# A decode attention kernel: K and V of a head fetched in three pieces instead of four, V's last piece multiplied ahead of the softmax, P transposed behind the next head's first keys

## The chip, the cores and the metric

One core of a Trainium2 chip. The metric is device microseconds of one execution; medians of several executions are given. The profile's **span** is shorter than that: it runs from the program's first instruction to its last.

## The reference

One token passes through attention with a cache of 65,536 keys (32 query heads, 8 key/value heads, 128 wide), then through a small gated feed-forward network.

```python
q = (layernorm(x) @ wq) -> [32 heads, 128]
scores = q . k_cache * 128**-0.5          # 8 x 65536 x 128, bf16
o = softmax(scores) . v_cache             # 8 x 65536 x 128, bf16
h = x + o @ wo
out = h + (sigmoid(layernorm(h) @ w_gate) * (layernorm(h) @ w_up)) @ w_down
```

K and V are 16.8 MB each per head, 268 MB for all eight; with the weights 282.33 MB must be read once.

## The kernel before

K and V travel through a ring of 128 KB a partition, in four slots of 32 KB. A 4 MB block of K is transposed on VectorE in eight chunks of 4 KB a partition (into `ktw`), and TensorE makes scores of it. After a head's four blocks come maxima, exponentials on ScalarE and the transposes of P on VectorE; V's blocks are multiplied in *rounds* of eight matmuls (two chunks each), one head behind. The code below is shortened, with lines joined and parts left out.

```python
order = [("wq", 0)] + [("K", b) for b in range(NR)]           # NR = 4 blocks a head
for b in range(NR, NB):
    order += [("K", b), ("V", b - NR)]
# a load waits until the block that was in its slot is used up:
def freed(ld): return {"wq": "q", "K": f"F{b}", "V": f"PV{b}"}[k]
# ...
if r == NR - 1: softmax(i)                 # TensorE: scores, softmax, then V's block
pv(v)
# ...
P.part = {"dve": ("A4", i)}; transposed(i) # VectorE: P's transposes right after the softmax
```

TensorE's program is a loop whose control its own sequencer runs (544 comparisons with jumps are among that sequencer's records in the trace): registers hold addresses (`p` into P, `v` into the ring), and jumps pick the pieces of code.

```python
label("values", "part")
e.reg_mov(m, NR); e.reg_mov(k, 0); e.reg_mov(v, v_even)
# ... jumps to the section of this part (V0, V1, V2, V3), each with its wait
goto("sums", "values")
pv_regs(e)                                 # 14 addresses from p and v
goto("products", "sums")
section("B")                               # 8 matmuls: one round
e.reg_alu(p, p, 2 * 512, ALU.add)
e.reg_alu(v, v, 2 * 2 * CH, ALU.add)
e.reg_alu(m, m, -1, ALU.add)
e.br_ne(m, 0, on_true="sums", on_false="sums_end")
label("sums_end")
away("br_ne", k, 0, "rest", rest, "products")     # the last round of V's last block, behind its own wait
```

`away(...)` is a comparison with a jump to code that lies elsewhere and comes back. In the last head two more things are done between the blocks of V: the output projection of the first seven heads (a section `L`, 28 matmuls called "rows" here), and a *column step* of four small products that turns its result by 90 degrees.

## Time and profile before

| | kernel before |
|---|---|
| time, median of 3 | 658.43 us (658.34 to 658.81) |
| span of the profiled execution | 657.1 us |
| packets of the data queue (q1) | 10,658 |
| last weights landed | 654.83 us |
| last values done | 644.17 us |

In the groups below, the columns are busy time, mean duration in ns of one, then the idle time ahead of them and what ended it.

```profile
L511 DVE STREAM_TRANSPOSE ktw<-ring 128x1024 f32<-128x1024 f32 x256 | 291.6, 1205 | 128.0 <-DMA ring<-in_A_k_cache_dram 128.0
L431 PE MATMUL PS<-ring,PT_sb 128*32 x1024 | 83.9, 455 | 23.6 <-issue 13.2
```

"issue" is time in which TensorE waited for nothing the profile can name. In views of the profile a q after an engine's name (PEq, PEldq, SPq) marks its sequencer.

### The profile page before, as it was taken

The numbers are of one execution on the slowest core, as the hardware profiler recorded it, in microseconds if no ns is written. First come the engines' busy times: TensorE is split into PE (matmuls) and PEld (weight loads), VectorE is DVE, ScalarE is ACT, GpSimd is POOL, SyncE is SP. The second block draws the span as 40 slices with busy tenths as digits, with TensorE's granted clock in tenths as the row PEclk, the third lists the DMA queues.
The fourth block names the chain that finished last, engine by engine and source line by source line (L and its number), as shares of the span: only waits on it lengthen the run. The fifth ranks groups of instructions, "written<-read, shape, count | busy, mean of one in ns | idle before, by whom it ended". The sixth has DMA issues, their size and how long they took to land. (4 is left out here: it accounts for less than half of the span.)

```text
span 657.1 us, 6111 instructions
## 1 busy us (share of the span) xinstructions
PE 420.5 (64%) x2315; PEld 74.1 (11%) x1547; DVE 349.7 (53%) x439; ACT 42.9 (7%) x114; POOL 3.6 (1%) x17
## 2 busy tenths in 40 slices
PE   0688488548666585576765575764866668556746
PEld 0200011011000010010100110101100001001322
DVE  2399775547537665347555374465743575542202
ACT  1100200020000200020000200002000100002001
POOL 1000000000000000000000000000000000000000
PEclk9989689677888697776966769765888869677676
DMA  9999999999999999999999999999999999999998
GB/s 383 447 433 429 439 423 431 431 447 415 447 415 447 437 425 447 415 447 419 443 441 421 447 415 447 423 439 443 419 447 415 447 427 435 445 417 427 435 430 352
DMA packets 10802, 282.34 MB, mean 430 GB/s; under 512 B 1329, under 2 KB 1330, under 8 KB 1842
## 3 DMA queue, kind: packets, MB, share of 16 engines
q1 hardware_dynamic: 10658, 282.33, 99.7%
q10 hardware_dynamic: 144, 0.00, 0.0%
HBM read 282.33 MB, written 0.00 MB: 430 GB/s over the span
## 5 line engine op out<-in xcount | busy, mean ns | idle before, releaser
L431 PE MATMUL PS<-ktw 128*128 128x512 bf16 x1024 | 299.9, 442 | 157.4 <-DVE ktw L511 153.6
L511 DVE STREAM_TRANSPOSE ktw<-ring 128x1024 f32<-128x1024 f32 x256 | 291.6, 1205 | 128.0 <-DMA ring<-in_A_k_cache_dram 128.0
L431 PE MATMUL PS<-ring,PT_sb 128*32 x1024 | 83.9, 455 | 23.6 <-issue 13.2
L431 PEld LDWEIGHTS PS<-ktw 128*128 x256 | 27.1, 106 | 408.2 <-issue 256.8
L565 DVE STREAM_TRANSPOSE PT_sb<-P_sb 128x512 bf16<-128x512 bf16 x32 | 20.2, 684 | 54.0 <-PE PS L602 52.3
L551 ACT ACTIVATE negmax<-PS 128x1 f32<-128x1 f32 x8 | 1.4, 171 | 520.6 <-PE PS L549 520.6
L431 PEld LDWEIGHTS PS<-ring,PT_sb 128*32 x1024 | 25.8, 116 | 79.8 <-issue 74.6
L516 DVE TENSOR_REDUCE M_sb<-PS 128x1 f32<-128x512 f32 x32 | 19.9, 684 | 25.5 <-PE PS L431 25.5
L555 ACT ACTIVATE P_sb<-PS,negmax 128x512 bf16<-128x512 f32 x32 | 21.6, 686 | 0.3
L572 DVE TENSOR_REDUCE lsum<-PS 128x1 f32<-128x4 f32 x8 | 1.3, 163 | 31.2 <-PE PS L570 31.2
L542 PE MATMUL PS<-identf,gm 128*1 128x128 f32 x16 | 3.4, 301 | 16.9 <-DVE gm L540 16.9
L616 DVE TENSOR_TENSOR Lw<-O,blk_of 128x896 bf16<-128x896 bf16 (+1 forms) x2 | 1.4, 683 | 20.6 <-ACT O L606 20.6
L402 PE MATMUL PS<-st,onesf 128*128 128x2 f32 x4 | 1.2, 362 | 16.1 <-DVE st L401 16.1
L431 PE MATMUL PS<-ring,xz 128*8 x32 | 9.2, 459 | 2.3 <-issue 2.3
L599 ACT ACTIVATE po_sb<-PS,rl 128x512 bf16<-128x512 f32 x8 | 5.5, 687 | 53.2 <-PE PS L431 53.2
L431 PE MATMUL PS<-ktw,O 128*1 x26 | 7.6, 464 | 0.0
L549 PE MATMUL PS<-one_f,gmrep 1*128 1x1 f32 x16 | 4.2, 330 | 5.0 <-DVE gmrep L546 5.0
L555 ACT ACTIVATION_READ_ACCUMULATOR P_sb<-PS,negmax 128x1 f32 x32 | 6.5, 202 | 0.0
L476 DVE STREAM_TRANSPOSE qt<-qh 32x512 bf16<-32x512 bf16 x1 | 0.7, 699 | 10.6 <-ACT qh L473 10.6
L602 PE MATMUL PS<-sel_bf,po_sb 128*128 128x4 bf16 x32 | 2.0, 168 | 6.4 <-ACT po_sb L599 6.4
L417 DVE CAST hT<-x_col 128x4 f32<-128x4 bf16 x1 | 0.2, 171 | 10.6 <-DMA x_col<-in_A_x_dram 10.6
L661 DVE COPY yr<-PS 1x512 f32<-1x512 f32 x1 | 0.7, 679 | 8.3 <-PE PS L659 8.3
(82 smaller groups left out, 74.0 us busy)
## 6 DMA issues: line engine op xcount, KB each, us to landing
ring<-in_A_k_cache_dram SPq DMA_DIRECT2D x32, 4096.0 KB, 28.7
ring<-in_A_v_cache_dram SPq DMA_DIRECT2D x31, 4096.0 KB, 26.4
ring<-in_A_wq_dram SPq DMA_DIRECT2D x1, 4096.0 KB, 12.3
ktw<-in_A_wo_dram SPq DMA_DIRECT2D x1, 3584.0 KB, 12.7
ring<-in_A_v_cache_dram SPq DMA_DIRECT2D x1, 3072.0 KB, 13.2
ring<-in_B_w_gate_dram SPq DMA_DIRECT2D x1, 1792.0 KB, 19.0
ring<-in_B_w_up_dram SPq DMA_DIRECT2D x1, 1344.0 KB, 21.7
ring<-in_A_v_cache_dram SPq DMA_DIRECT2D x1, 1024.0 KB, 15.2
```

Of the source, the lines that this page charges most:

```text
L431: return e.add_instruction(mybir.InstMatmult(name=nc.get_next_instruction_name(), engine=mybir.EngineType.PE, ins=[rhs, lhsT], outs=[e.low ...
L511: op("dve", lambda e, d=dst, sr=src: e.transpose(d, sr), deps, f"T{b}.{c}", to="T")
L516: op("dve", lambda e, u=u: e.tensor_reduce(M_sb[:, u % 4:u % 4 + 1], ps(u % NS, 0, 512), AX.X, ALU.max), [f"S{b}.{NC - NR + k}"], f"mx{u}" ...
L542: op("pe", lambda e: e.matmul(ps(MISC, 0, 128, 0, 1), lhsT=gm[:, :], rhs=identf[:, :], start=True, stop=True), [f"gm{h}"], f"gmT{h}", to="Q")
L549: op("pe", lambda e: e.matmul(ps(MISC, 128, 129), lhsT=gmrep[0:1, :], rhs=one_f[0:1, 0:1], start=True, stop=True), [f"gmrep{h}"], f"neg{h}")
L551: op("act", lambda e: e.activation(negmax[:, k:k + 1], ps(MISC, 128, 129), AF.Copy, scale=-att_scale), [f"neg{h}"], f"negmax{h}")
L555: op("act", lambda e, b=b: e.activation(P_sb[:, (b % 4) * 512:(b % 4 + 1) * 512], ps(b % NS, 0, 512), AF.Exp, bias=negmax[:, k:k + 1], sca ...
L565: op("dve", lambda e, b=b: e.transpose(PT_sb[:, (b % 4) * 512:(b % 4 + 1) * 512], P_sb[:, (b % 4) * 512:(b % 4 + 1) * 512]), [f"E{b}", f"o ...
L572: op("dve", lambda e: e.tensor_reduce(lsum[:, :], ps(MISC, 132, 136), AX.X, ALU.add), [f"l{h}"], f"ls{h}", to="D")
L599: op("act", lambda e: e.activation(po_sb[:, :], ps(PO, 0, 512), AF.Copy, scale=rl[:, :]), [f"PV{NR * h + NR - 1}", f"rl{h}"], f"po{h}", to ...
L602: op("pe", lambda e, t=t: e.matmul(ps(OX, 0, 4), lhsT=po_sb[:, t * 128:(t + 1) * 128], rhs=sel_bf[:, 8 * t:8 * t + 8:2], start=(t == 0), s ...
L616: op("dve", lambda e: e.tensor_tensor(Lw[i][:, :].rearrange("p (j c) -> p j c", j=n), bass.AP(tensor=O2, offset=j0, ap=[[NQ, 128], [1, n], ...
```

## The change

Its intent: fewer and longer transfers. A head's K comes as 48, 32 and 48 KB a partition, and so does V. V's first two pieces (48 and 32) are multiplied in one run of ten rounds after the next head's first score block, the last piece in six rounds ahead of the next head's softmax. P's transposes move behind the next head's first eight key chunks.

```diff
+PIECES = ((0, 12), (12, 20), (20, 32))           # chunks of 4 KB
+AT = {"K": (0, 0, 8), "V": (12, 24, 20), "K0": (0, 12, 20), "V7": (0, 12, 20), "wq": 24, "wg": 0, "wd": 7}
+for h in range(1, HKV):
+    load("K", h, 0, ["F0.1" if h == 1 else f"F{h - 1}.3"], "ka", f"K{h}.0")
+    load("V", h - 1, 0, ["F0.3" if h == 1 else f"PV{h - 2}.3:2"], "va", f"V{h - 1}.0")
+    load("V", h - 1, 1, ["F0.4" if h == 1 else f"PV{h - 2}.3"], "vb", f"V{h - 1}.1")
+    load("K", h, 1, [f"F{h}.0"], "ka", f"K{h}.1")
+    load("K", h, 2, [f"F{h}.1", f"PV{h - 1}.0:4"], "kb", f"K{h}.2")
+    load("V", h - 1, 2, [f"PV{h - 1}.0"], "vb", f"V{h - 1}.2")
 ... (V of the last head, then the output projection's weights, then V's last piece as 32 + 16 KB, then the network's weights)
 
-for p in ("A0", "B0", "A1", "A2", "A3", "A4"):   # VectorE; A4 is P's transposes
+for p in ("A0", "A4", "B0", "A1", "A2", "A3"):
 
-PARTS: four parts of four rounds
+PARTS = {0: 10, 3: 6}
+step = (2 * 2 * 512, 2 - 2 * 2 * 512)
 goto("sums", "values")
 pv_regs(e)
+away("br_eq", p, c, "waits", waits, "products")  # in every round: is it the one before which to wait?
 goto("products", "sums")
 section("B")
-e.reg_alu(p, p, 2 * 512, ALU.add)
+e.reg_alu(p, p, s, ALU.add)
+e.reg_alu(s, s, step[0] ^ step[1], ALU.bitwise_xor)
 e.reg_alu(v, v, 2 * 2 * CH, ALU.add)
 e.reg_alu(m, m, -1, ALU.add)
 e.br_ne(m, 0, on_true="sums", on_false="sums_end")
```

The three new lines in the round (one of them takes the place of a line) are in the diff because chunks now lie in the ring in their natural order, so the step in P alternates, and because the wait for the second piece falls in the middle of a run.

## The prediction

> **What bounds the kernel now.** I read the page's head first, then the waits of the compute engines against those of the DMA-issuing queue, then the timeline of one head and of the last 17 us.
>
> ```profile
> span 657.1 us, 6111 instructions
> DMA  9999999999999999999999999999999999999998
> GB/s 383 447 433 429 439 423 431 431 447 415 447 415 447 437 425 447 415 447 419 443 441 421 447 415 447 423 439 443 419 447 415 447 427 435 445 417 427 435 430 352
> q1 hardware_dynamic: 10658, 282.33, 99.7%
> ```
>
> The sixteen DMA engines are busy in every one of the forty slices, 99.7% of the span on one queue. 282.33 MB have to come in whatever the program does. The packet records of the trace have the first packet 1.07 us after the start and the last of the down-projection's weights at 654.6 us, so between them the engines never rest. (415 against 447 in a slice is only how many whole packets begin in it.)
>
> ```profile
> DVE ktw L511 <- DMA ring<-in_A_k_cache_dram: 128.0, 14, 10.4
> ...
> SPq L365 <- DVE scr L512: 324.2, 30, 19.4
> SPq L365 <- PE PS L431: 222.4, 29, 18.8
> ...
> DMA to landing us min/median/max: 14.6/27.5/39.7
> ```
>
> VectorE waits for keys (128.0 us, 14 times). The DMA-issuing queue waits for VectorE and TensorE too, 546 us of it, but these waits cost nothing: a 4 MB piece needs 9.7 us on the engines, and even the fastest of 63 landed 14.6 us after its issue, so it lay queued behind another for some 4 us; the median lay 17 us. VectorE (53%) and TensorE (64%) have room.
>
> ```profile
> 221.51 9.09 DVE L511 STREAM_TRANSPOSE ktw<-ring 128x1024 f32<-128x1024 f32 x8
> 222.76 0.61 PE L431 MATMUL PS<-ktw 128*128 128x512 bf16 x1 [3.76 <-DVE ktw L511]
> ...
> 234.75 0.28 PE L570 MATMUL PS<-L_sb,lsel 128*128 128x4 f32 x2
> 234.96 2.16 PE L431 MATMUL PS<-ring,PT_sb 128*32 x32
> ```
>
> Here are the prices for the work between transfers: eight key chunks are transposed in 9.1 us; their 32 score matmuls take 222.76 to 234.75, 12.0 us, in the bad case where the TensorE was idle before; four rounds of values 2.16 us.
>
> ```profile
> 640.17 2.72 PE L431 MATMUL PS<-ring,PT_sb 128*32 x24
> 643.26 0.91 PE L431 MATMUL PS<-ring,PT_sb 128*32 x8 [0.37 <-PEq L169]
> 644.23 0.69 ACT L599 ACTIVATE po_sb<-PS,rl 128x512 bf16<-128x512 f32 x1 [35.95 <-PE PS L431]
> 653.58 1.68 PE L831 MATMUL PS<-ring,hhT 128*1 128x128 bf16 x56 [0.98 <-DVE hhT L826]
> 655.31 0.57 ACT L839 ACTIVATE y_sb<-PS 1x128 bf16<-1x128 f32 x2 [4.23 <-PE PS L831]
> 655.96 0.33 SPq L841 DMA_DIRECT2D out_dram<-y_sb  x1
> ```
>
> At the end two chains nearly tie: the last values (643.26 to 644.17) with 9.4 us of small steps up to the last matmuls at 653.58; and the last weights, whose semaphore is complete at 654.83, after which only 0.45 us of matmuls are left.
>
> [...] one engine starts a 32 KB packet each 1.2091 us (mean from 50 to 580 us), which is 433.6 GB/s for sixteen. [...] 24 KB packets come each 0.9082 us, 28 KB each 1.0588, 32 KB each 1.2091. The slope is 0.3009 us for 8,192 bytes, and what is left over is 5.6 ns a packet. [...] the trace shows 0.50 from 221 to 230 us and 1.00 after 233, so I take the 12.0 us above as the price of a score block.
>
> **The change part by part.** Bytes, matmuls, chunk transposes and exponentials stay the same in number.
>
> First, fewer and longer packets. A head's K, like its V, was four rows of 32 KB a partition and becomes 48, 32 and 48. At the slope above a 48 KB row is 1.805 us and 5.6 ns, so 1.811. A partition's 128 KB then take 2 x 1.811 + 1.209 = 4.831 us against 4 x 1.2091 = 4.836: one overhead of 5.6 ns saved. An engine serves 8 partitions, and there are 16 such tensors: 128 x 5.6 ns = 0.72 us. In the loop a 4 MB piece lands each 9.68 us against 8 x 1.2091 = 9.673; those 7 ns or so at each boundary, 16 boundaries fewer, are 0.1 us. Gain: 0.8 us, on the path that sets the end.
>
> Second, the new order of freeing and loading. It costs only where an issue comes too late. I lay one head out from the first byte of its first K piece; pieces take 14.5 or 9.7 us, land 0.3 us after their end (the last weights did: 654.56 to 654.83), and have to be issued 1.1 us ahead (first issue at 0.0, first packet at 1.07). Landings: K first 14.8, V first 29.3, V second 39.0, K second 48.6, K last 63.1, V last 77.6, and the period is 77.3. Eight transposes end at 23.9: this frees K's second piece, needed at 37.5 (13 us to spare). P's four transposes follow (4 x 0.684, to 26.7); scores end at 14.8 + 1.2 + 12.0 = 28.0; then the sums, and four more transposes to 33.2 free K's last piece, needed at 47.2. The ten rounds of values end soon after V's second piece, 39.0 + 4 x 0.9 = 42.6; V's last is needed at 61.7. Chunks 12 to 19 run from 48.6 and 20 to 23 from 63.1 to 67.7; this frees the next head's first K, needed at 76.2: 8.5 us to spare, the least in the loop. The last eight end at 76.8, scores at 80, two rounds of values at 82: next V first, needed at 90.7. So no wait reaches the engines in the loop; the 2.7 us of P's transposes were off the path and still are, as is the softmax after V's last.
>
> Third, the start is tighter. VectorE begins at 29.0 as now (the query's projection sets that). K's last piece needs the query's weights out of the way: 27.8 against 33.8. Next head's first K needs 12 transposes: 42.7 against 48.3. First V: 56.2 against 62.8. K second of head 1: transposes may begin at 71.6, as P's come after, so 80.7 against 87.0. K last of head 1: scores from 75.6 (when the head's weights are in place) plus 12.0, sums, four transposes: 92.7 against 96.6. The least there is 3.9 us.
>
> Fourth, the tail. V's last transfer waits for ten rounds, which wait for V's second: 616.8 + 3.9 = 620.7; the output projection's weights run behind V's second until 626.3, so 4.5 us to spare. V's last 16 KB land at 641.98 - 0.8 = 641.2, with two rounds to do instead of one: 2 x 0.9 + 0.2 = 643.2, against 644.17 now, since the column step that kept the TensorE busy until 640.1 moves ahead. That chain gains 1.0, the weights 0.8; the lesser counts. Sum: 658.43 - 0.8 = 657.6.
>
> **The rivals.** A wait takes the place: a late issue starves the engines. For it: the ring holds only 128 KB[...], the spare falls to 3.9 us at the start[...]. Against: 8.5 us in the loop. Once at the start it makes 658 to 661; for 2%, 13.2 us, each head would have to lose 1.7 us, so its longest stretch would have to be wrong by 10. Second: 48 KB rows don't travel as one packet, or at another pace. Cut in three of 16 KB they cost 3 x (0.6018 + 0.0056) = 1.822, not 1.811, 11 ns x 256 = 2.8 us more than reckoned: 660.4. Against: 32 KB rows go whole. [...] Third: the last chain binds, if the two rounds after the last landing take longer than reckoned: the gain shrinks to 0.2 or so, 658.2. Fourth, upward: the first seven landings after 60 us come each 9.72 us rather than 9.68; were that a boundary cost, up to another 0.5 us would go: 657.1.
>
> **Range and chances.** The centre moves to 657.7 for the bubbles at the start; 656.9 below by the fourth rival, 659.6 above by the first and second. Faster by 2% would need 13 us from a stream that is never idle: 0.01. Slower by 2% needs a starved loop: 0.04. Within 2%: 0.95.
>
> **What would show it.** DMA nines in all slices; packets down by 2,048 to about 8,600, 48 KB ones each 1.81 us an engine; busy share still 99% or more; no issue-to-landing time under 10.8 us for a 4 MB piece or 15.6 for a 6 MB one; last weights landing near 654.0. I am wrong if a slice falls to 8 or less between 40 and 640 us, if the packet count doesn't fall, or if the last matmuls start well after the last weights are in.

The forecast's sum came to 658.43 - 0.8 = 657.6 us, and the centre to 657.7.

## More of the kernel before

For the kernel before, span and time differ by 1.3 to 1.5 us in most executions.

Of the 10,658 packets 1,185 have 4 bytes only, about 16 for each transfer.

## The result and the profile after

| | before | after |
|---|---|---|
| time, median | 658.53 us (658.34 to 658.81, 4 runs) | 659.88 us (658.85 to 660.26, 4 runs) |
| span of the profiled execution | 657.1 us | 658.4 us |
| mean span of all timed executions in the next call, on chip 0 | 656.93 us | 658.20 us |
| packets of the data queue (q1) | 10,658 | 8,354 |
| last weights landed | 654.83 us | 654.23 us |
| last values done | 644.17 us | 646.4 us |

The ratio of the fast runs is 1.0018 (95% interval 1.0000 to 1.0035); a ratio here is the mean time of one kernel's fast runs over that of the other's of the same rounds, so not quite the ratio of the medians. The change makes the kernel 1.3 us slower, where 0.8 us faster was predicted. That is 0.2%, so by a limit of 2% both count as the same, and everything below is about differences of that size.

The page of the changed kernel, then its waits and those of the DMA-issuing queue:

```profile
span 658.4 us, 6290 instructions
DMA  9999999999999999999999999999999999999997
q1 hardware_dynamic: 8354, 282.33, 99.3%
...
DVE ktw L496 <- DMA ring<-in_A_k_cache_dram: 162.3, 20, 16.3
...
SPq L324 <- DVE scr L499: 306.9, 18, 24.1
SPq L324 <- PE PS L415: 199.5, 21, 19.6
...
DMA to landing us min/median/max: 14.5/25.7/35.4
...
L415 PE MATMUL PS<-ring,PT_sb 128*32 x1024 | 101.3, 485 | 70.4 <-PEq L171 35.5
```

The engines are still busy in every slice, with 2,304 packets fewer: 2,048 of data, as predicted, and 256 of 4 bytes. The 48 KB rows travel as one packet each, 3,968 in all, and an engine starts one each 1.812 us (median), where 1.811 was reckoned. Only the last digit fell, from 8 to 7: something in the last 16 us goes on without transfers. Issues still come well ahead of need: the fastest piece landed 14.5 us after its issue, the median 25.7. From one landing to that of the same piece a head later the median went from 77.45 us to 77.40 in this trace and 77.36 in a second one of the changed kernel. So the stream itself got faster, and the last weights came 0.6 us earlier (0.9 in the second trace). The matmuls of the rounds, however, now have 70.4 us of idle time ahead of them instead of 23.6. Yet from the landing of the last weights to the end of the span there are now 658.42 - 654.23 = 4.2 us, against 657.12 - 654.83 = 2.3 before.

The chain that ended last, and the timeline of the tail, after:

```profile
by line: PE PS L415 0.8%; issue 0.5%; PE PS L798 0.5%; PE PS L816 0.1%; DVE hh L808 0.1%; PE PS L616 0.1%; ACT po_sb L584 0.1%; DVE hhT L811 0.1%; PE PS L386 0.1%; DVE y_sb L822 0.1%; DVE Lw L600 0.0%; PE PS L587 0.0%; PE PS L606 0.0%; ACT 
...
634.67 2.02 PE L651 MATMUL PS<-one_f,yr 1*128 1x1 f32 x8 [0.77 <-DVE yr L645]
639.16 4.44 PE L415 MATMUL PS<-ring,PT_sb 128*32 x32 [2.48 <-PEq L171]
644.66 0.63 PE L415 MATMUL PS<-ring,PT_sb 128*32 x8 [1.06 <-issue]
645.77 0.64 PE L415 MATMUL PS<-ring,PT_sb 128*32 x8 [0.48 <-issue]
646.45 0.69 ACT L584 ACTIVATE po_sb<-PS,rl 128x512 bf16<-128x512 f32 x1 [39.02 <-PE PS L415]
655.53 0.95 PE L816 MATMUL PS<-ring,hhT 128*1 128x128 bf16 x56 [1.29 <-DVE hhT L811]
656.54 0.57 ACT L824 ACTIVATE y_sb<-PS 1x128 bf16<-1x128 f32 x2 [3.48 <-PE PS L816]
657.18 0.33 SPq L826 DMA_DIRECT2D out_dram<-y_sb  x1
```

The column step (634.67) ends at 636.7. V's last piece had landed in its two parts at 636.52 and 641.38. But the first of the six rounds starts only at 639.16, the fifth at 644.66, and the values are done at 646.4. The matmuls over the last weights start at 655.53, 1.3 us after these weights are in; the prediction had named that as a sign of being wrong. The end is now set by TensorE's tail.

What TensorE did in the gaps is in its sequencer's records. First those of one window of the tail after (duration in ns: least, median, most), then of the same stretch of the kernel before:

```profile
L712 PEldq ALU_OP  x6: 43/43/43, 639.2 to 645.8; - x6
L713 PEldq ALU_OP  x6: 36/36/36, 639.3 to 645.9; - x6
L714 PEldq FUSED_REGOPS  x5: 42/42/42, 639.4 to 644.9; - x5
L716 PEldq COMPARE_BRANCH  x5: 214/226/226, 639.5 to 645.0; - x5
L657 PEldq COMPARE_BRANCH  x11: 72/75/222, 635.0 to 645.6; - x11
L567 PEldq FUSED_REGOPS  x18: 42/79/79, 638.7 to 645.5; - x18
```

```profile
L580 PEldq FUSED_REGOPS  x18: 42/74/74, 634.0 to 642.6; - x18
L721 PEldq FUSED_REGOPS  x6: 51/51/51, 634.4 to 643.3; - x6
L724 PEldq COMPARE_BRANCH  x6: 72/140/214, 634.5 to 643.4; - x6
```

Before, a round takes the sequencer three fused register operations for the addresses (L580), one fused operation for all three steps (L721), and the loop's comparison (L724). After, there are an added operation (L712, the step from a register), another (L713, the exclusive or) that are recorded singly beside the fused rest (L714), and a comparison in front of the products (L657). From the start of one record to the start of the next, in one round each:

```text
after  639.030 compare L657 | +0.154 step L712 | +0.104 xor L713 | +0.147 fused L714 | +0.100 compare L716 (taken)
       | +0.284 +0.138 +0.137 three fused L567 | +0.100 compare L657 at 640.194        -> 1.16 us a round
       the round after it: 640.194 to 641.308                                          -> 1.11 us
before 640.193 fused L721 | +0.160 compare L724 (taken) | +0.273 +0.132 +0.133 three fused L580
       | +0.125 fused L721 at 641.016                                                  -> 0.82 us a round
```

Over the whole trace (medians) the two added operations cost 0.10 us each, the second 0.15 in the first round above, and the comparison 0.15, even though it doesn't jump: 0.35 us a round.

A slower TensorE clock is not the reason. These windows (the last three columns are the granted clock, the share of the DMA engines and GB/s) hold the first four of the six rounds and the last two:

```profile
639.00:643.40 4.40, 3.95 (x32) 0.67 (x32) 0.00 (x0) 0.00 (x0) 0.00 (x0) 0.50 1.00 430
643.50:646.40 2.90, 1.36 (x20) 0.32 (x16) 0.00 (x0) 0.00 (x0) 0.00 (x0) 1.00 1.02 435
```

The rounds follow each other every 1.11 to 1.16 us at half the clock, and the last follows the fifth after 1.11 us (644.66 to 645.77) at the full clock. Over the whole traces a round at half the clock takes 1.12 us (median, from the starts of the matmuls), in the kernel before 0.85. So TensorE gets its work no faster than the sequencer hands it out.

Over the whole traces, before and after, 0.13 and 0.15 us pass until the sequencer's next record when a comparison does not jump, and 0.27 and 0.28 us when it does (medians).

### The profile page after: what moved, and what is told of

It reads as the page before. It is cut to its first block, busy times and chain, and to the rows that moved or that the text cites. A ratio compares the mean times of both kernels' runs of the same rounds, so it can differ in the third digit from the quotient of the medians.

```text
span 658.4 us, 6290 instructions
## 1 busy us (share of the span) xinstructions
PE 427.0 (65%) x2315; PEld 69.1 (10%) x1547; DVE 350.2 (53%) x432; ACT 42.9 (7%) x114; POOL 3.6 (1%) x17
## 3 DMA queue, kind: packets, MB, share of 16 engines
q1 hardware_dynamic: 8354, 282.33, 99.3%
## 5 line engine op out<-in xcount | busy, mean ns | idle before, releaser
L415 PE MATMUL PS<-ktw 128*128 128x512 bf16 x1024 | 288.0, 432 | 112.5 <-DVE ktw L496 101.2
L415 PE MATMUL PS<-ring,PT_sb 128*32 x1024 | 101.3, 485 | 70.4 <-PEq L171 35.5
L415 PEld LDWEIGHTS PS<-ring,PT_sb 128*32 x1024 | 21.3, 116 | 147.2 <-issue 145.9
L531 DVE TENSOR_REDUCE gmj<-PS 1x4 f32<-1x128 f32 x8 | 2.2, 279 | 43.8 <-PE PS L529 43.8
```

Source lines behind the costliest of these rows:

```text
L415: return e.add_instruction(mybir.InstMatmult(name=nc.get_next_instruction_name(), engine=mybir.EngineType.PE, ins=[rhs, lhsT], outs=[e.low ...
L531: op("dve", lambda e: e.tensor_reduce(gmj[:, :], ps(MISC, 0, 128, 0, 1).rearrange("p (i a c) -> p a i c", a=4, c=NC), AX.XY, ALU.max), [f" ...
```

## The experiments

**Theory A**: the three sequencer instructions in each round make rounds long. **A'**: the 2.5 us before the first of the last rounds are jumps through two empty parts. **Rival B**: the two rounds behind V's last landing set the end, as the prediction's third rival had it. **Rival C**: TensorE's clock, which the windows above rule out for the changed kernel. All were timed in five rounds; the kernel before ran 9 to 11 times beside them. The first three kernels ran on chip 0, the next four on chip 1 and the last three on chip 15; the changed kernel was repeated on chip 0 alone, so later differences from it are between chips on which the kernel before agrees within 0.05 us of span.

| kernel | median, us | before, same chip | mean span | span of before |
|---|---|---|---|---|
| changed kernel again | 659.57 | 658.40 | 658.20 | 656.93 |
| wait outside the rounds | 659.38 | 658.40 | 657.56 | 656.93 |
| last piece smaller | 660.29 | 658.40 | 659.02 | 656.93 |
| before with the three instructions | 662.70 | 658.37 | 661.07 | 656.93 |
| straight to the values | 658.46 | 658.37 | 656.96 | 656.93 |
| pairs of rounds | 660.89 | 658.37 | 657.17 | 656.93 |
| pairs and straight | 661.18 | 658.37 | 656.28 | 656.93 |
| straight and outside | 657.53 | 658.38 | 656.22 | 656.98 |
| outside, padded | 659.26 | 658.38 | 656.32 | 656.98 |
| rows of 24 KB | 659.01 | 658.38 | 657.72 | 656.98 |

**The changed kernel again** (no edit).

> The changed kernel once more, as the yardstick on this chip. All theories: 1 to 1.5 us slower than the kernel before (659.5 to 660.2). In its tail the value rounds of the last head follow each other every 1.15 us (0.8 us in the kernel before), the first starts some 2.5 us after the column step ends, and the last weights land near 654.2.

As expected: 659.57 us (659.03 to 660.34), ratio 1.0019 (1.0005 to 1.0032).

**The wait out of the rounds.** The run is cut in two loops, as the kernel before had it for its last round.

```diff
-e.reg_mov(m, PARTS[0])
+e.reg_mov(m, 6); e.reg_mov(k, 4)
-away("br_eq", p, c, "waits", waits, "products")
 ...
 label("sums_end")
+away("br_ne", k, 0, "waits", waits, "sums")      # waits, sets m to k and k to 0, and goes round again
```

> The comparison that the change put into every round of values is moved out of the loop (a second loop for the rounds behind the wait, as the kernel before had it). Theory A, the comparison in each round makes the rounds long: rounds every 0.8 us instead of 1.15, the last values end near 644.5 instead of 646.4, the end is then set by the last weights, and the time is 658.1, 1.8 under the changed kernel. Rival B, the last 16 KB piece needs two rounds after landing: no change in the round's pace that matters, 659.9. Rival C, TensorE clock: no change, 659.9.

A miss in the time, which hardly moved (659.38 us, from 658.21 to 660.26), and half a hit in the span, which fell 0.64 us, less than expected. In the profiled execution the rounds start at 638.19, 639.19, 640.16, 641.18, so a round takes 1.0 us, not 0.8. The sequencer's records give the reason: the comparison is only 0.15 of the 0.35 us, the two register operations remain.

**The last piece smaller.** One round instead of two behind the last landing.

```diff
-LAST = [(20, 28), (28, 32)]
+LAST = [(20, 30), (30, 32)]
-e.reg_alu(c, c, 8, ALU.add)
+e.reg_alu(c, c, 8 + step[0], ALU.add)
```

> V's last piece of the last head is split 40 KB and 8 KB instead of 32 and 16, so one round of values follows the last landing instead of two. Theory A (rounds and jumps are slow, the piece has long landed when its rounds begin): no change, 659.9 within 0.3. Rival B (two rounds behind the last landing set the end): one round less on the path, 0.8 to 1.15 us faster, 658.8 to 659.0.

Rival B falls: with one round less behind the last landing the kernel did not get faster; it was 0.7 us slower than the changed kernel. That A expected no change is a miss too. The first part, now 40 KB, landed at 638.46, and the sequencer left its wait at 638.49, when it had come to it at 638.1. So 0.4 us were waited there. But in this profiled execution, the fastest of the five, the values are done at 646.4 as in the changed kernel's, and the spans are 658.3 and 658.4. Where the other executions lost the 0.8 us of mean span the trace does not show; they spread over 1.5 us.

**The three instructions put into the kernel before.**

```diff
 pv_regs(e)
+away("br_eq", m, 99, "never_so", lambda: None, "products")
 goto("products", "sums")
 section("B")
-e.reg_alu(p, p, 2 * 512, ALU.add)
+e.reg_alu(p, p, s, ALU.add)                       # s holds 2 * 512
+e.reg_alu(s, s, 0, ALU.bitwise_xor)
```

> The kernel before, with the changed kernel's three extra sequencer instructions put into each round of values: the step added from a register, an exclusive or on that register, and a comparison that never jumps. Transfers, their order and all else as before. Theory A (these three make the rounds longer and the tail late): last head's rounds every 1.1 to 1.15 us instead of 0.8, last values end 1.2 to 1.5 us later (645.4 to 645.7), last weights unmoved at 654.8, time 659.2 to 659.6 against 658.4. Rival (the new order of transfers and waits makes the tail late, not the rounds): 658.4 to 658.6.

The rounds are as expected: 628.92, 630.02, 631.16, 632.26, so 1.1 us. The rest is a miss: the time rose by 4.3 us, about four times as much as expected, and the last weights, expected unmoved, landed at 658.43 instead of 654.83. Timeline and windows of this kernel's tail (in the windows the last two columns are the share of the DMA engines and GB/s):

```profile
631.16 2.15 PE L431 MATMUL PS<-ring,PT_sb 128*32 x16 [0.40 <-issue]
633.35 0.80 SPq L362 DMA_DIRECT2D ring<-in_A_v_cache_dram  x2
...
626.00:631.00 5.00, 2.70 (x21) 0.64 (x20) 0.68 (x1) 0.00 (x0) 0.00 (x0) 0.94 0.97 419
631.00:636.00 5.00, 2.73 (x24) 0.48 (x24) 0.00 (x0) 0.00 (x0) 0.00 (x0) 0.50 0.42 118
636.00:641.00 5.00, 3.57 (x28) 0.50 (x24) 0.00 (x0) 0.00 (x0) 0.00 (x0) 0.50 1.01 433
```

V's last transfer waits for rounds, and they now end at 633.3 instead of 626.4. By then the queue has run dry: 118 GB/s in these 5 us. A late issue cost the stream itself some 3.6 us, which is the prediction's first rival, in a kernel that I had not thought of. It shows two things: the three instructions lengthen the rounds with the old order of transfers too, so the order is not what makes rounds long; and the old order has less spare for slow rounds than the new one. It does not show how the changed kernel's tail gets late, as the lateness here came in another way, by a dry queue. That is left to the repairs below, which keep the new order.

**Straight to the values.** This one only sets the part counter.

```diff
-away("br_eq", w, w0 - 4, "rows_of_o", lambda: section("L"))
+away("br_eq", w, w0 - 4, "rows_of_o", lambda: (section("L"), e.reg_mov(w, w0 - 12)))
```

> The changed kernel, but after the column step of the last head the part counter is set so that the TensorE goes straight to the last part of values instead of through two empty parts. Theory A' (the 2.5 us before the first of the last rounds are some ten comparisons and jumps): the gap falls to about 1, rounds stay at 1.15 us, time 658.2 to 658.5 against the changed kernel's 659.6 to 659.9. If the gap is a wait for the landing of V's piece: gap and time stay.

A hit, and the largest single one: one register move takes 1.24 us off the span. Timeline of its tail:

```profile
635.22 2.02 PE L651 MATMUL PS<-one_f,yr 1*128 1x1 f32 x8 [0.77 <-DVE yr L645]
637.17 0.63 PE L415 MATMUL PS<-ring,PT_sb 128*32 x8
```

The first round now follows the column step without a gap. In the changed kernel the sequencer had run 15 comparisons and jumps, nine of them taken, from 634.68 to the wait at 638.50, 3.8 us; the column step's matmuls hide only the first 2.0 us of it.

**Pairs of rounds.** The loop body holds two rounds, so the step in P is a constant again, as in the kernel before, whose three steps made one fused record (L721, 0.11 us); the wait is out of the rounds.

```diff
+for second in range(2):                            # 16 matmuls in the body, addresses set twice
     ...
-e.reg_alu(p, p, s, ALU.add); e.reg_alu(s, s, step[0] ^ step[1], ALU.bitwise_xor)
-e.reg_alu(v, v, 2 * 2 * CH, ALU.add)
+e.reg_alu(p, p, 2, ALU.add); e.reg_alu(v, v, 2 * 2 * 2 * CH, ALU.add)
```

> The changed kernel with the loop body holding two rounds: one comparison and one fused register step per two rounds, no register-held step, no comparison for the wait inside. Theory A: a round takes 0.65 to 0.75 us, the last values end 2 to 2.5 us earlier, the last weights then set the end, time 657.9 to 658.2. Without theory A: 659.6.

In the span the direction is right (1.03 us less), though a round took 0.85 us, not 0.65 to 0.75. The trace says why: from 640 to 645 us the clock granted to TensorE was 0.50, and its 48 matmuls kept it busy for 4.90 of these 5.00 us. Over the whole trace a round takes 0.85 us at half the clock and 0.44 at the full one (medians). With the sequencer out of the way TensorE itself sets the pace, which the expectation had left out. The time is a clear miss: 660.89 us, from 658.82 to 663.28. The difference between time and span was 2.0 to 5.1 us in its six executions, where the changed kernel has 1.4 to 1.7.

**Pairs and straight.** Both edits.

> Both of the last two. Theory A and A': the tail of values is no longer on the path, the end follows the last weights (653.8 to 654.2) by the same 2.2 us as in the kernel before, and the saved packet overhead shows: 657.5 to 657.9, 0.5 to 0.9 us under the kernel before. If something else holds the tail: 658.4 or more.

A miss in the time (661.18 us) by the same split: the span came to 656.28, 0.65 under the kernel before, with 2.3 to 5.1 us after it. So the repairs work within the span, and something outside the program's own span takes the gain away.

**Straight and outside.** The two repairs that lengthen no code: straight to the values, wait out of the rounds.

> Changed kernel with two repairs that lengthen no code: no comparison inside the rounds, and the straight way from the column step to the last values. Theory A with A': the program's span is 656.3 to 656.5 (before 656.9, changed 658.2), set by the last weights, and [...] the time after the span stays 1.4 us: 657.7 to 657.9, some 0.6 under the kernel before. If the repairs don't add up: 658.4 or more.

A hit, a little better than expected: 657.53 us (657.50 to 657.98) against 658.38 (658.08 to 659.06), ratio 0.9987. Its interval, 0.9974 to 1.0001, just reaches 1, but the five executions lie all under the nine of the kernel before. The two repairs add up: 0.64 and 1.24 us of span alone, 1.98 together. The span ends 1.4 us before the time, as in the kernel before. Its chain and its last matmuls:

```profile
by line: DMA ring<-in_B_w_down_dram 4.4%; PE PS L415 0.6%; issue 0.2%; SPq L350 0.2%; SPq L355 0.1%; SPq L324 0.1%; DVE y_sb L824 0.1%; PE PS L818 0.0%
...
641.66 0.63 PE L415 MATMUL PS<-ring,PT_sb 128*32 x8 [0.91 <-DMA ring<-in_A_v_cache_dram]
653.90 0.28 PE L818 MATMUL PS<-ring,hhT 128*1 128x128 bf16 x8 [0.24 <-DMA ring<-in_B_w_down_dram]
```

Now the sequencer comes to the wait for V's last piece just as it lands (640.99), and at the very end TensorE waits for the last weights: the chain is a chain of transfers again, which is what the prediction had taken for granted.

**Outside, padded.** Twenty idle register operations (19 in the built program) in the section that waits for the output projection's weights.

```diff
-lambda: (section("L"), ...)
+lambda: ([e.reg_alu(w, w, 0, ALU.bitwise_xor) for _ in range(20)], section("L"), ...)
```

> The same with twenty idle register steps more in the TensorE's program, done once in the last head while it waits for the output projection's weights, so that its code is as long as in the two kernels with paired rounds. Theory L (what follows the span grows with the length of the TensorE's program[...]): span unchanged within 0.2, but 2 to 5 us after it instead of 1.4, time 659 to 661. If length has nothing to do with it: 657.7 to 657.9 like the unpadded one.

A hit: span 656.32, but 2.7 to 3.6 us after it, 659.26 us. Nineteen more instructions, without any effect in the span, cost about 1.7 us behind it. The trace has a 16,384-byte packet of the kind "instruction" at 655.33 that the unpadded kernel's trace lacks; the two kernels with pairs have one too, and so has the profiled execution of the kernel before, at 658.42, one of its few with 2.3 us behind the span. But the kernel with rows of 24 KB below, whose transfer-issuing program is longer, has such a packet at 656.53 and only 1.3 us behind its span, so it alone doesn't decide the matter. That these nineteen instructions cost time behind the span is shown. Whether they do so by the program's length, by where later code comes to lie, or in another way, is not. The changed kernel itself has 1.4 to 1.7 us behind its span, so this is no cause of its slowness.

**Rows of 24 KB.** Packets alone: straight and outside, with each 48 KB row fetched as two of 24.

```diff
 def load(k, h, q, deps, sem, name, cols=None):
     ...
+    if (z - a) > 8 or (k, h, q, z) == ("V", HKV - 1, 2, 28):
+        mid = (a + z) // 2
+        dma("sp", ... chunks a to mid ..., sem, deps)
+        a, deps = mid, ()
     dma("sp", ... chunks a to z ..., sem, deps, name)
```

> The same as straight_and_outside, but each 48 KB row is fetched as two rows of 24 KB (32 KB of the very last as two of 16), so an engine has some 256 packets more. Theory of packets (5.6 ns each, and about 0.2 us for 32 more boundaries): last weights land 1.4 to 1.7 us later, span 657.8 to 658.1. If packets cost nothing: span as straight_and_outside, 656.4.

A hit in the last weights; the span, 657.72, is just under the range. Packets of the page rise from 8,354 to 12,962 (4,096 of data, 512 of 4 bytes):

```profile
q1 hardware_dynamic: 12962, 282.34, 99.8%
```

The last weights land at 655.43 instead of 653.86, 1.57 us later, and the span grows 1.50. For some 256 packets more an engine that is 6.1 ns each, boundaries included. The packet step of the prediction holds.

## Why the prediction was right or wrong

- **What bounds the kernel**: right. The stream fills the span before and after (99.7% and 99.3% of it).
- **First part, packets**: right. Last weights 0.6 us earlier in one trace and 0.9 in the other, where 0.8 was reckoned, against a single trace of the kernel before. The second rival falls with it: 48 KB packets go whole, each 1.81 us, and the changed kernel's 16 KB packets, each 0.607 us, fit the 5.6 ns a packet as well. (The first packet starts at 1.03 us, not 1.07; nothing rests on it.) The experiment with halved rows, its opposite, gave 1.57 us for 1.4 to 1.7 expected.
- **Second and third part, order and start**: right. First K of head 1 was issued at 43.2 (42.7 reckoned), first V at 56.7 (56.2), head 1's second K at 80.9 (80.7) and last at 90.2 (92.7). V's last transfer of the last head went out at 622.06 instead of 620.7, because the ten rounds before it were slow, and the 4.5 us to spare covered that. No slice between the first and the last fell below 9.
- **Fourth part, the tail**: this step failed. It had the values done at 643.2, and they were done at 646.4. V's last 16 KB landed at 641.38, as reckoned (641.2). The two rounds took 1.76 us from 644.66, as reckoned (2 x 0.9). What was wrong is the start: the prediction let them begin at the landing, as if TensorE stood waiting. It came 3.3 us late. Three terms were missing. The way from the column step through two empty parts delays the first round 2.5 us; four rounds at 1.15 us, where I had carried 0.9 from the profile before; and 0.9 us for the jump to the last wait between the fourth and the fifth. Together they are 4.4 us (2.5 + 4 x 0.25 + 0.9), of which 1.1 us would have been spent waiting for the landing anyway. I had priced the new waits and transfers of the diff, but its register operations and comparisons at nothing.
- **The third rival** was right that the last chain would bind, but gave the wrong reason (two rounds instead of one behind the landing; refuted by the smaller last piece) and about a quarter of the size: 0.6 us over the centre (658.2) instead of 2.3.
- **The first rival** had named jumps too, but as a danger to the transfers. They hurt the tail: 15 comparisons and jumps, 3.8 us, ahead of its first round.
- **The centre** of 657.7 is where the kernel goes when the tail is mended: 657.53 for straight and outside. That the time would stay within 2% came true without the tail being right: no mistake of this size could have broken it.
- **Left open**: the 0.8 us of span that the smaller last piece lost, by what way more instructions delay what follows the span, and why this takes sometimes 2 and sometimes 5 us in the kernels with paired rounds.

## What to carry to other kernels

Transfers set the pace here, and in the changed kernel the loop forgave a slow sequencer and the tail didn't: with rounds of 1.12 us instead of 0.85 (at half the clock) a piece still landed 77.40 us after that of the head before (77.45), but the span grew by 1.3 us. In the tail the three added instructions lay on the path, 0.35 us in each round. So price the control instructions of a diff too, from the sequencer's records of the profile before, and look at which instruction the engine's queue will come to first when the data lands. Judge a small edit by span as well as by time, because in three kernels here a program with more code lost behind its span what it had gained inside. And when the sequencer is out of the way, look at the clock: with paired rounds TensorE needed 0.85 us a round at half of it, 0.44 at the full one.
